# Second layer of a mixture of experts: one third of its token tiles by seven half-width products

## The chip, the cores and the metric

The kernel runs on one NeuronCore of a Trainium2 chip. Its engines run their own instruction queues in order: TensorE (PE: matmuls, with their weight loads shown apart as PEld), VectorE (DVE), ScalarE (ACT), GpSimd (POOL) and SyncE (SP), which here issues the DMAs. Matmul results land in PSUM, eight banks of 128 partitions x 2 KB; GpSimd works on SBUF alone in this kernel. The metric is the device time of one execution in microseconds (us), the median over runs.

## What is computed

Two parts follow each other. The first is a gated linear recurrence over 768 tokens for 4 batches of 8 heads of 48; the second a dense mixture of 8 experts over the 3072 tokens of 384 features that come out of it:

```python
for t in range(S):
    state = f[:, :, t, :, None] * state + np.einsum('bhd,bhe->bhde', k[:, :, t], v[:, :, t])
    y[:, :, t] = np.einsum('bhd,bhde->bhe', q[:, :, t], state)
...
for e in range(E):
    h = np.maximum(x @ w1[e], 0.0)
    ye = h @ w2[e]
    out += P[:, e:e + 1] * ye
```

x has 384 features, h has 1024, and P comes from the gate by eight rounds of normalising rows and columns. All inputs are 32-bit. The kernel keeps that precision with 16-bit matmuls by splitting each operand into a high and a low 16-bit part and taking three products: high x high, low x high, high x low. So one exact-looking product of two blocks is three matmuls.

## The kernel before

**Stages.** From 0 to some 490 us the recurrence runs, with experts 0 and 1 as fillers (`raw_pairs`, `moe_tile`, `moe`), and then the gate's normalising rounds. From 492 us to the end 48 steps run, and the change lies in them. A step n is one entry of `ORDER`: an expert e of 2 to 7, a half m of its 1024 hidden features (512, in two blocks c of 256 as they are stored, each again two blocks f of 128), and a batch b of 768 tokens. The tokens of a batch are two halves v of 384, each three tiles t of 128; a matmul of the first layer takes tile t of both halves together, 256 columns.

**First layer of a step (`period`).** h = x @ w1 for three row blocks of features by two of hidden units by three of tokens would be 18 block products; here it is 15, a fast matrix multiplication. `SLOTS` lists them: product number, bank (A to F), whether the bank is begun anew. Each slot issues 6 matmuls of 256 columns (two c, three split parts). What is to be combined between products is in `EVENTS`: after slot s a bank is copied to SBUF by ScalarE ('copy'), VectorE adds a copy to a bank in place ('add') or writes bank plus copy to a new copy ('sum'), and when a bank is complete ScalarE writes its positive part in 16 bits ('hh') and VectorE the remainder ('hl'). The six banks end as the six (f, t) blocks of h: A (0,0), B (1,0), E (0,1), D (1,2), F (0,2), C (1,1). Events past slot 14 run in the first slots of the next step (`pending`). The sums of weight blocks are made by GpSimd in `prepare_w1`, those of x in `convert`.

**Second layer (`layer2`).** For each tile t and half v a result of 128 tokens x 384 features is summed in one PSUM bank over f, c and the three split parts: 12 matmuls of 384 columns; six results, 72 matmuls a step. Two banks (pool `psm`) alternate. When a result is complete it is scaled by its token's P and added to the accumulator `acc`, either by VectorE from PSUM in one instruction, or by ScalarE into SBUF and then GpSimd; two of six go the first way. This generator belongs to the step before: while step n runs its slots, `period` draws 72/15 matmuls of step n-1's second layer behind each slot. In the first step there is none, and the last one's run alone at the end.

**Other work in the slots (`plan`).** Each (n, s) can hold jobs: the next group's weights (`prepare_w1`: load, GpSimd sums, three high parts on ScalarE, three low parts on VectorE; `prepare_w2`: load, one high part of 768 columns, two low parts of 384), the results of experts 0 and 1 that were stored early and are added back (`readds`, line 1137, on VectorE or on ScalarE and GpSimd), and checks of the inputs' range (`all_checks`, line 1155: it loads all 64 weight blocks once more and takes their largest value on VectorE, then samples q, k and v in `guard`, then `verdict`). If a check fails, `general`, a slow form, runs behind the fast one.

**Order.** `mm` (line 277) chains all matmuls in the order of the program and `pin` does so for each other engine, so no engine takes an instruction ahead of an earlier one. An instruction waits for what it reads, and a bank or tile is written anew only when its readers are done; readers of one bank on two engines also go one after the other.

Of the kernel before, what the change touches and what calls it, by code (L numbers as in the profile page):

```python
# [19 lines left out]
C = 64  # L20
HS = S // 2
# [22 lines left out]
XW1_MAX = 65000.0 / DM  # L44
W2_MIN, W2_MAX = 2.0 ** 4, 2.0 ** 15
# [27 lines left out]
ORDER = [(e, m, b) for e in range(2, NE) for m in range(2) for b in range(B)]  # L73
STEPS = 8
# [175 lines left out]
def fast(ctx, tc, qkf, vbd, wg, w1, w2, out, flag):  # L250
# [83 lines left out]
    def load(e, k, j):  # L334
        src = (w1 if k == 1 else w2)[e, j]
        n = 4 * (k - 1) + j
        if n < 6:
            raw = xp.tile([128, 1152], F32, name=f"w{k}r_{e}_{j}", tag=f"x{'hl'[n % 2]}{3 - n // 2}", bufs=1)[:, 0:768]
        else:
            raw = rp.tile([128, 768], F32, name=f"w{k}r_{e}_{j}", tag="wraw")  # L340
# [430 lines left out]
    def guard():  # L771
# [8 lines left out]
        def load_qk(n):  # L780
            t = lp.tile([128, 768], F32, name=f"qks{n}", tag="wmax", bufs=2)[0:R, 0:512].rearrange("r (i m t) -> r i m t", i=8, m=2)
# [5 lines left out]
        def load_v(n):  # L787
            t = lp.tile([128, 768], F32, name=f"vs{n}", tag="wmax", bufs=2).rearrange("s (i e) -> s i e", i=8)
# [7 lines left out]
        before = None  # L796
        for n in range(9):
            now = (load_qk if n < 4 else load_v)(n % 4) if n < 8 else None
            if before:
                pin(nc.vector.tensor_reduce(out=before[1], in_=before[0], axis=AX.X, op=ALU.max, apply_absolute_value=True))  # L800
            before = now
            yield
# [194 lines left out]
    k1, k2 = {}, {}  # L997

    def prepare_w1(e, j):
        raw = rp.tile([128, KT, 256], F32, name=f"k1r_{e}_{j}", tag="wraw")  # L1000
        nc.sync.dma_start(out=raw, in_=w1[e, j])
# [9 lines left out]
        for r, p, op, q in WSUMS:  # L1011
            pin(nc.gpsimd.tensor_tensor(out=block(r), in0=block(p), in1=block(q), op=ALU.add if op == '+' else ALU.subtract))  # L1012
# [15 lines left out]
    def prepare_w2(e, j):  # L1028
        raw = rp.tile([128, 2, DM], F32, name=f"k2r_{e}_{j}", tag="wraw")
        nc.sync.dma_start(out=raw, in_=w2[e, j])  # L1030
        yield
        wh, wl = (lp.tile([128, 2, DM], F16, name=f"k2{n}_{e}_{j}", tag=f"k2{n}", bufs=4) for n in "hl")
        pin(nc.scalar.activation(out=wh, in_=raw, func=AF.Copy, scale=W2S))
        yield
        for g in range(2):
# [3 lines left out]
            yield  # L1039

# [62 lines left out]

    def layer2(n, h):
# [3 lines left out]
        for t in range(TT):  # L1108
            for v in range(2):
                u = 2 * b + v  # L1110
                ps = psm.tile([128, DM], F32, name=f"kyps_{n}_{t}_{v}", tag="m")
                i = 0
                for f in range(2):
                    for c in range(2):
                        wh, wl = k2[e, 2 * m + c]
                        hh, hl = h[f, t]
                        for a, w in ((hh, wh), (hl, wh), (hh, wl)):
                            mm(out=ps, lhsT=a[:, c, 128 * v:128 * v + 128], rhs=w[:, f, :], start=(i == 0), stop=(i == 11))
                            i += 1
                            if i < 12:  # L1120
                                yield
                y = acc[b][:, v, t, :]
                p = pes[:, u * TT + t, e:e + 1]
                if n == first[b]:
                    pin(nc.scalar.activation(out=y, in_=ps, func=AF.Copy, scale=p))
# [29 lines left out]
    def all_checks():  # L1155
        todo = [(e, j, k) for e in range(NE) for k in (1, 2) for j in range(4)]
        raws_ = []
        for i in range(len(todo) + 1):
# [8 lines left out]
            yield  # L1167
        yield from guard()
        yield from verdict()

    plan = {}

    def at_slots(n, slots, gen):
# [142 lines left out]
```

## Time and profile before

| what | value |
|---|---|
| median of 3 runs | 1544.53 us (1544.12 to 1544.67) |
| span of the profiled execution | 1542.9 us |
| instructions | 32479 |
| TensorE clock over the span, mean granted | 0.996 of full speed |

The profile gives no other time of the profiled execution than its span, from its first to its last instruction; the runs' median is 1.6 us longer.

```profile
core 0: 1542.9 us, clock 0.996
```

How to read it: busy time is the union of an engine's instructions, in us, with its share of the span. A matmul's record covers its way through the array, so records of successive matmuls overlap, and the distance from start to start is what a matmul costs in a full queue. Rows of groups give line, engine, operation, what is written from what by the program's names (kyps is a result of the second layer, kb_A a bank of the first, kh and kl the two parts of h, k1 and k2 the weights of the two layers, cp a copied bank, yt and acc an evicted result and the accumulator), shapes, count, then busy us, mean ns of one, and idle time of the engine before it with what ended it. Line 278 is the helper that issues every matmul.

### The profile page before, as it was taken

To read this page: it belongs to the slowest core of one execution; us is meant where nothing else is said; L and a number is where in the kernel's file an instruction comes from. 1 tells how busy PE (TensorE), PEld (TensorE's weight loads), DVE (VectorE), ACT (ScalarE), POOL (GpSimd) and SP (SyncE) were. 2 spreads that over 40 slices of the span, in tenths; PEclk is the share of its full clock that TensorE was granted. 3 is DMA by queue.
4 is the path that set the end of the run, shared out by engine and by line. 5 is a ranking of instruction groups with operands and counts; after the bars stand their busy time and mean duration, and the time that the engine had idled before them with its cause. 6 is when DMAs were issued, how large, how long until landed. Compare 5 with 4: busy or idle time off the path is not lost.

```text
span 1542.9 us, 32479 instructions
## 1 busy us (share of the span) xinstructions
PE 1518.7 (98%) x13454; PEld 1104.3 (72%) x13454; DVE 1091.6 (71%) x1810; ACT 775.2 (50%) x1489; POOL 517.0 (34%) x656
## 2 busy tenths in 40 slices
PE   7999999999999999999999999999999999999998
PEld 5788876676666777777777777777777777777775
DVE  8888888984774667666767677666766666665554
ACT  6655556553344655555544554445444454445432
POOL 1244434545527112333333332222322232222211
PEclk9999999999999999999999999999999999999999
DMA  9455555531002122222222222111212112100011
GB/s 270 113 134 133 124 137 122 141 95 29 32 32 78 31 83 78 69 87 67 83 73 88 72 78 63 52 62 42 64 50 62 44 39 57 31 12 11 6 57 65
DMA packets 89678, 114.39 MB, mean 74 GB/s; under 512 B 50640, under 2 KB 67152, under 8 KB 89520
## 3 DMA queue, kind: packets, MB, share of 16 engines
q1 hardware_dynamic: 89520, 112.22, 26.1%
q8 instruction: 107, 1.75, 0.5%
q14 instruction: 51, 0.42, 0.1%
HBM read 88.41 MB, written 14.16 MB: 66 GB/s over the span
## 4 chain that ended last, share of the span: by engine, by line
PE 91%; DVE 5%; ACT 2%; POOL 1%; issue 1%; DVEq 0%; ACTq 0%; POOLq 0%
PE kyps L278 36%; PE yps L278 12%; PE hps L278 9%; PE kb_A L278 8%; PE kb_B L278 8%; PE kb_D L278 6%; PE kb_C L278 4%; PE kb_E L278 2%; PE kb_F L278 2%; PE kvps L278 1%; PE aps L278 1%; POOL xs L965 1%; PE wps L278 0%; DVE w2l L350 0%; POOL k1s L1012 0%
## 5 line engine op out<-in xcount | busy, mean ns | idle before, releaser
L1131 POOL TENSOR_TENSOR acc<-acc,yt 128x384 f32<-128x384 f32 x172 | 173.3, 1008 | 629.7 <-ACT yt L1130 629.7
L278 PE MATMUL kyps<-k2h,kl 128*128 128x384 f16 x1152 | 375.6, 326 | 0.0
L278 PE MATMUL kyps<-k2h,kh 128*128 128x384 f16 x1152 | 375.6, 326 | 0.0
L278 PE MATMUL kyps<-k2l,kh 128*128 128x384 f16 x1152 | 375.6, 326 | 0.0
L278 PEld LDWEIGHTS <-k1h 128*128 128x128 f16 x2880 | 281.5, 98 | 70.4
L278 PEld LDWEIGHTS <-kh 128*128 128x128 f16 x2304 | 225.4, 98 | 103.9
L1130 ACT ACTIVATE yt<-kyps,pes 128x384 f32<-128x384 f32 x172 | 99.8, 580 | 323.0 <-PE kyps L278 321.1
L278 PEld LDWEIGHTS <-k1l 128*128 128x128 f16 x1440 | 140.7, 98 | 63.2 <-issue 5.7
L1127 DVE SCALAR_TENSOR_TENSOR acc<-kyps,pes,acc 128x384 f32<-128x384 f32 x92 | 56.8, 617 | 171.7 <-PE kyps L278 171.7
L278 PEld LDWEIGHTS <-kl 128*128 128x128 f16 x1152 | 112.7, 98 | 44.7
L1224 ACT ACTIVATE cp<-kb_A 128x512 f32<-128x512 f32 x144 | 86.0, 597 | 86.0 <-PE kb_A L278 85.4
L278 PE MATMUL yps<-w2h,hl 128*128 128x384 f16 x384 | 125.8, 328 | 3.1 <-DVE hl L431 3.0
L278 PE MATMUL yps<-w2l,hh 128*128 128x384 f16 x384 | 125.9, 328 | 1.0 <-DVE w2l L350 1.0
L278 PE MATMUL yps<-w2h,hh 128*128 128x384 f16 x384 | 125.8, 328 | 0.2 <-ACT hh L428 0.2
L278 PEld LDWEIGHTS <-w1h 128*128 128x128 f16 x1344 | 97.1, 98 | 35.2 <-issue 4.3
L1224 ACT ACTIVATE cp<-kb_B 128x512 f32<-128x512 f32 x144 | 87.0, 604 | 50.3 <-DVE kb_B L1226 50.2
L278 PEld LDWEIGHTS <-hh 128*128 128x128 f16 x768 | 74.7, 98 | 47.3 <-issue 2.3
L1229 DVE TENSOR_TENSOR cp<-kb_D,cp 128x512 f32<-128x512 f32 x144 | 98.7, 685 | 12.8 <-PE kb_D L278 11.8
L278 PE MATMUL hps<-xh,w1h 128*128 128x128 f16 (+1 forms) x672 | 83.6, 257 | 1.6 <-DVE hl L382 1.5
L278 PE MATMUL hps<-xl,w1h 128*128 128x128 f16 (+1 forms) x672 | 84.0, 257 | 1.1 <-DVE xl L640 0.6
L278 PE MATMUL hps<-xh,w1l 128*128 128x128 f16 (+1 forms) x672 | 84.6, 257 | 0.1
L278 PE MATMUL kb_A<-xbh,k1h 128*128 128x256 f16 x288 | 78.5, 273 | 0.2 <-ACT cp L1224 0.2
(244 smaller groups left out, 3439.4 us busy)
## 6 DMA issues: line engine op xcount, KB each, us to landing
wm<-in_w_dram SPq DMA_DIRECT2D x64, 384.0 KB, 3.1
q<-in_qkf_dram SPq DMA_DIRECT2D x23, 672.0 KB, 5.4
vr<-in_vbd_dram SPq DMA_DIRECT2D x24, 384.0 KB, 3.6
ys<-yr SPq DMA_DIRECT2D x48, 192.0 KB, 2.8
k1r<-in_w_dram SPq DMA_DIRECT2D x24, 384.0 KB, 3.0
k2r<-in_w_dram SPq DMA_DIRECT2D x24, 384.0 KB, 3.0
yb<-ys SPq DMA_DIRECT2D x48, 192.0 KB, 2.4
out_dram<-acc SPq DMA_DIRECT2D x24, 192.0 KB, 1.9
```

The source lines that it names most:

```text
L278: ins = (nc.tensor.transpose if transpose else nc.tensor.matmul)(**kw)
L965: pin(nc.gpsimd.tensor_tensor(out=block(r), in0=block(p), in1=block(q), op=ALU.add if op == '+' else ALU.subtract))
L1127: pin(nc.vector.scalar_tensor_tensor(out=y, in0=ps, scalar=p, in1=y, op0=ALU.mult, op1=ALU.add))
L1130: pin(nc.scalar.activation(out=yt, in_=ps, func=AF.Copy, scale=p))
L1131: pin(nc.gpsimd.tensor_tensor(out=y, in0=y, in1=yt, op=ALU.add))
L1224: pin(nc.scalar.activation(out=fresh(ev[2]), in_=bk, func=AF.Copy))
L1229: pin(nc.vector.tensor_tensor(out=fresh(ev[4]), in0=bk, in1=old, op=ALU.add if ev[2] == '+' else ALU.subtract))
```

## The change

The middle token tile, t = 1, of each step is taken out of the plain scheme. Its 256 tokens (two halves v) by 256 hidden units of a c block (two f) are seen as a 2 x 2 block matrix A, and the weights, two f by two halves of the 384 features (192 each), as a 2 x 2 block matrix B. The eight block products of A B become seven, with four sums of blocks of A, four of B, and sums of the products. Three split parts and two c each: 42 matmuls of 192 columns take the place of 24 of 384. The other two tiles stay as they were: 48 matmuls of 384.

- *Left sums*: when bank E (f = 0, t = 1) is complete, ScalarE writes its positive part as 32-bit ('hs') and the high part of block A11 ('ga'); VectorE makes four sums of blocks from the banks E and C and SBUF ('gs'), and A11's low part ('gb'); ScalarE writes the sums' high parts ('gh') and GpSimd their low parts ('gl'). E's own 'hh' and 'hl' go.
- *Right sums*: `prepare_pairs` loads each w2 block a second time, makes four sums of 192 columns on GpSimd, a high part of 768 columns on ScalarE and a low one on VectorE, once in four steps for each c.
- *Results* (`paired`): two banks hold two half-width sums each. Three are copied by ScalarE to SBUF, GpSimd makes two sums of the copies, VectorE one from PSUM, and these are added to the banks in PSUM by VectorE (192 columns for one half v, 384 for the other), after which the two results are evicted; the second one's add and eviction come one and two slots later.
- *Order of the second layer*: plain results (0, 2) first, then the pair. It begins at slot 2 of the next step (`LAG`), not at slot 0, and is drawn by units: a plain matmul counts 1, a narrow one 0.51, and a pause of 5 at the end. In the last step the pair comes before the last plain result, and banks of the first layer serve as rooms.
- *Plan*: all early results go by ScalarE and GpSimd; the weights' largest values are taken from the blocks that are loaded anyway (experts 0 and 1 are loaded for it in `first_maxima`); slots of the weight preparation move; the verdict moves to the last four steps. In a slot a step's own events now come before those left from the step before.
- Two limits of the checks are halved, since sums of blocks are larger, and the buffers for raw weights become three.

```diff
+          14: (('sum', 'D', '-', 4, 3), ('hs', 'E'), ('hh', 'D', 1, 2)), 15: (('add', 'C', '+', 3), ('ga', 'E'), ('hh', 'C', 1, 1), ('gs', 'E', 0)),
+          16: (('gs', 'C', 1), ('gs', 'E', 2), ('gs', 'C', 3)), 17: (('hl', 'C', 1, 1), ('add', 'F', '+', 10)),
+          18: (('gh', 0, 2), ('hh', 'F', 0, 2)), 19: (('gl', 0, 2), ('hl', 'F', 0, 2)), 20: (('gh', 2, 4), ('hl', 'D', 1, 2)), 21: (('gl', 2, 4), ('gb', 'E'))}
...
+        def product(out, left, right, start=False, stop=False):
+            for c in range(2):
+                if left is None:
+                    a = [x[:, c, :] for x in h['a']]
+                elif left[0] is None:
+                    a = [x[:, left[1], c, :] for x in h['g']]
...
+                for i, (x, y) in enumerate(((a[0], w[0]), (a[1], w[0]), (a[0], w[1]))):
+                    mm(out=out, lhsT=x, rhs=y, start=start and c == 0 and i == 0, stop=stop and c == 1 and i == 2, skip_group_check=True)
+                    yield PAIR_COST
+
+        def paired(t=PAIRED):
...
+            yield from product(x0, None, (0, 0), start=True)
+            yield from product(x1, (None, 1), (None, 1))
+            copy(0, x0)
+            yield from product(y0, (None, 0), (None, 0), start=True)
+            copy(1, x1)
+            yield from product(y1, (None, 2), (None, 2))
+            copy(2, y0)
+            pin(nc.gpsimd.tensor_tensor(out=part[:, 1, :], in0=part[:, 1, :], in1=part[:, 2, :], op=ALU.add))
+            pin(nc.gpsimd.tensor_tensor(out=both[:, 1, :], in0=part[:, 0, :], in1=part[:, 1, :], op=ALU.add))
+            yield from product(x0, (1, 0), (1, 0))
+            pin(nc.vector.tensor_tensor(out=both[:, 0, :], in0=y1, in1=part[:, 0, :], op=ALU.add))
+            yield from product(x1, (None, 3), (1, 1), stop=True)
+            yield from product(y0, (1, 1), (None, 3), stop=True)
+            pin(nc.vector.tensor_tensor(out=x1, in0=x1, in1=both[:, 0, :], op=ALU.add))
+            evict(t, 0, px, True)
+
+            late = n < len(ORDER) - 1
+            postpone(late, lambda: pin(nc.vector.tensor_tensor(out=py, in0=py, in1=both, op=ALU.add)))
+            postpone(2 * late, lambda: evict(t, 1, py, False))
+            yield PAUSE
...
-            at_slots(n, (0, 2, 7, 11, 13), gen)
-            at_slots(n + 1, (5, 6, 8), gen)
+            at_slots(n, (0, 5, 5, 6, 9, 11, 13), gen)
+            at_slots(n + 1, (11, 13, 14) if not n % 4 else (4, 6, 8), gen)
...
+        elif kind == 'gs':
+            f, n = hs['f'], ev[2]
+            v, other, op = ((1, 4, ALU.subtract), (1, 5, ALU.add), (0, 1, ALU.subtract), (0, 2, ALU.add))[n]
+            pin(nc.vector.scalar_tensor_tensor(out=f[:, n], in0=bk[:, :, 128 * v:128 * v + 128], scalar=0.0, in1=f[:, other], op0=ALU.max, op1=op))
...
+            for ev in EVENTS.get(s, ()):
+                event(ctxt, ev)
             for ev in pending.pop(0) if pending else []:
                 event(*ev)
-            for ev in EVENTS.get(s, ()):
-                event(ctxt, ev)
+            due()
             for job in plan.pop((n, s), []):
                 job()
-            for _ in range(72 * (s + 1) // PRODUCTS - 72 * s // PRODUCTS):
-                next(lower, None)
+            if s == LAG and n:
+                lowers.append(layers.pop(0))
+            drain((24 * len(PLAIN) + 42 * PAIR_COST + PAUSE) / PRODUCTS)
```

262 lines of the change are left out of this document (183 added, 79 removed), and 2 rows, old and new, of the table EVENTS.

## The prediction, made before the change was run

> **What bounds the kernel now.** I read the busy shares first, then the chain that ended last, then TensorE's own waits in the stage that changes, then that stage in windows.
>
> ```profile
> span 1542.9 us, 32479 instructions
> PE 1518.7 (98%) x13454; PEld 1104.3 (72%) x13454; DVE 1091.6 (71%) x1810; ACT 775.2 (50%) x1489; POOL 517.0 (34%) x656
> PE 91%; DVE 5%; ACT 2%; POOL 1%; issue 1%; DVEq 0%; ACTq 0%; POOLq 0%
> PE kb_A L278 <- ACT cp L1224: 0.7, 3, 0.3
> PE kb_C L278 <- ACT cp L1224: 0.2, 1, 0.2
> 700.00:900.00 200.00, 199.80 (x1493) 145.78 (x1492) 140.62 (x222) 104.48 (x198) 72.69 (x101) 1.00 0.25 75
> 900.00:1100.00 200.00, 200.00 (x1501) 146.60 (x1500) 136.87 (x216) 97.19 (x182) 61.55 (x90) 1.00 0.20 59
> 1100.00:1300.00 200.00, 200.00 (x1503) 146.72 (x1501) 134.68 (x216) 95.59 (x180) 53.18 (x77) 1.00 0.19 53
> ```
>
> TensorE is busy 98% of the span and makes 91% of the chain. The two wait rows are all that it waited from 560 us to the end: 0.9 us. In the three windows (length, then busy time of PE, weight loads, VectorE, ScalarE, GpSimd, then clock) it is never idle, at full clock. So in the 48 steps time is a sum of matmul issue intervals; the other engines only have to keep up. They were busy 412, 297 and 187 of these 600 us.
>
> **What the narrower matmuls save.** A busy TensorE hides the interval, so it is read from starts and from merged pieces.
>
> ```profile
> 1523.15 12.53 PE kyps L278 x77
> 135.84 0.83 PE L278 MATMUL hps<-xh,w1h 128*128 128x128 f16 x12
> 136.51 0.83 PE L278 MATMUL hps<-xl,w1h 128*128 128x128 f16 x12
> 899.93 0.27 PE L278 MATMUL kb_B<-xah,k1h 128*128 128x256 f16 x1
> 900.47 0.27 PE L278 MATMUL kb_B<-xal,k1h 128*128 128x256 f16 x1
> ```
>
> 384 columns: 12.53/77 = 162.7 ns. 128 columns, each with another weight tile: (136.51-135.84)/12 = 55.8 ns. 256 columns: five intervals in 0.54 us, 108 ns. A matmul of 192 columns is not in the trace; halfway between 55.8 and 108 lies 82 ns, and the three known widths lie on one line, so I take 82.3. Bounds: 56 (no narrower than 128) and 108 (no wider than 256). A step has 90 matmuls of 256 columns and 72 of 384; the change turns 24 of the latter into 42 of 192: 24 x 162.7 - 42 x 82.3 = 3905 - 3457 = 0.448 us. Over 48 steps that is **21.5 us**, if nothing new waits.
>
> **A rule against it.** The Trainium skill, page "TensorE: Matmul & The Clock Gate", section "Back-to-back issue gap", says that in a stream of weight-load and matmul pairs one matmul costs about 81 ns at 128 columns and 131 ns at 512. By a line through these figures, an estimate, 42 half widths would cost 1.0 us a step more than 24 full ones. The rows above say 55.8 ns at 128 columns and 162.7 at 384, so here the trace speaks against that rule.
>
> **What the other engines gain in work.** Rows that price it:
>
> ```profile
> L278 PE MATMUL kyps<-k2h,kh x1152: 322/326/327, 505.0 to 1535.0; 128*128 128x384 f16 x192
> L1234 DVE SCALAR_TENSOR_TENSOR kl<-kb_E,kh 128x512 f16<-128x512 f32 x48 | 32.6, 679 | 0.0
> L1127 DVE SCALAR_TENSOR_TENSOR acc<-kyps,pes,acc 128x384 f32<-128x384 f32 x92 | 56.8, 617 | 171.7 <-PE kyps L278 171.7
> L1036 DVE SCALAR_TENSOR_TENSOR k2l<-k2r,k2h 128x384 f16<-128x384 f32 x48 | 26.2, 547 | 0.0
> L1023 DVE SCALAR_TENSOR_TENSOR k1l<-k1r,k1h x48: 410/548/1079, 452.6 to 1426.7; 128x256 f16<-128x256 f32 x24, 128x384 f16<-128x384 f32 x24
> L1149 DVE SCALAR_TENSOR_TENSOR acc<-yb,pes,acc 128x384 f32<-128x384 f32 x19 | 14.5, 766 | 1.3 <-POOL acc L1131 1.3
> L1224 ACT ACTIVATE cp<-kb_A 128x512 f32<-128x512 f32 x144 | 86.0, 597 | 86.0 <-PE kb_A L278 85.4 <-DVE kb_A L1226 0.3
> L1033 ACT ACTIVATE k2h<-k2r 128x768 f16<-128x768 f32 x24 | 20.4, 850 | 0.0
> L1152 ACT ACTIVATE yz<-yb,pes 128x384 f32<-128x384 f32 x29 | 17.6, 606 | 0.0
> L1131 POOL TENSOR_TENSOR acc<-acc,yt 128x384 f32<-128x384 f32 x172 | 173.3, 1008 | 629.7 <-ACT yt L1130 629.7
> L1012 POOL TENSOR_TENSOR k1s<-k1r,k1s 128x128 f32<-128x128 f32 x120 | 56.0, 467 | 3.8
> L737 POOL TENSOR_TENSOR al<-am,ah x21: 1157/1267/1678, 82.7 to 360.9; 128x512 f16<-128x512 f32 x21
> 1004.48 0.68 DVE L1234 SCALAR_TENSOR_TENSOR kl<-kb_E,kh 128x512 f16<-128x512 f32 x1
> 1005.07 0.68 DVE L1234 SCALAR_TENSOR_TENSOR kl<-kb_D,kh 128x512 f16<-128x512 f32 x1
> ```
>
> VectorE, per step: four left sums and the low part of A11, 256 columns at 0.41 each (the least of L1023), +2.05; the low part of E goes, -0.68; two half-width adds at 0.34 (410 less 64 columns at the 1.05 ns of (679-547)/128), +0.68; the full add in PSUM, +0.62; the low part of the paired weights, 768 columns in one step of two, about 0.95/2, +0.48; 19 early results move to ScalarE and GpSimd, -0.30. Together +2.85. The 64 weight maxima stay as many. A step now: from the first kyps at 505.0 to 1535.2 lie 47 steps and 72 matmuls more (11.7 us), so 21.67 us. Before: 412/600 x 21.67 = 14.9; after 17.7 of 21.2, 84%. A left sum reads PSUM and writes 32-bit; at most it costs the 0.62 of 384 columns, which would add 1.0 more (89%).
> ScalarE: E as a wide copy and a 256-column head for its high part (+0.4), two high parts of 512 (+1.2), three copies of 192 (about 0.35 each, +1.05), half a paired weight (+0.43), 0.4 early results (+0.24): +3.3 on 10.7, 66%. GpSimd: two low parts of 512 at 1.27, two half adds at 0.60 (between 467 and 1008), four weight sums of 0.60 every other step, 0.4 early results: +5.3 on 6.8, so 57%.
> No engine passes TensorE in the sum. DMA falls: the 64 weight loads that served the maxima alone become 24 for the pairs and 16 for the first two experts.
>
> **Where a queue could be late.** Order is pinned, so what counts is slack at the places where TensorE needs a bank again. A slot is 21.0/15 = 1.40 us (90 x 108 + 48 x 162.7 + 42 x 82.3 = 21.0). Queued VectorE work starts 0.59 us apart (1004.48, 1005.07), 0.09 below its duration.
> (a) Slots 0 to 5. VectorE now queues, ahead of the add into A: add C, a left sum, the x1 add and its eviction, three more left sums, the full add, low of C, add F. That is 0.60+0.33+0.27+0.5+1.2+0.5+0.6+0.6 = 4.6 us from the start of slot 0, and 0.5 where it must wait for the last pair product. The add starts near 5.1; the chain from there:
>
> ```profile
> 494.99 0.71 DVE kb_A L1226
> 495.72 0.61 ACT cp L1224
> 496.37 0.82 PE kb_A L278 x6
> ```
>
> 1.38 us from add to matmul: 6.5 against slot 5 at 7.0, slack 0.5 us. The low part of C ends near 4.6 against slot 4 at 5.6.
> (b) Slots 4 to 7 where a w2 block is prepared (two steps of four): ScalarE runs the first eviction (ready 6.8), a high part, the w2 high part (0.85 alone, 0.73 queued) and an early result before the copy of A that slot 7 needs: it ends near 9.6, slot 7 starts at 9.8. Slack 0.2 us.
> (c) Slots 9 and 10: copy of B at 11.7 against 12.6, the sum in D at 13.05 against 14.0.
> GpSimd's worst step (n%4 = 0) has 18 us of work; its sums for the last full add come 2 us into the next step, where VectorE reaches that add at 3.4.
> So steady steps should hold, barely. I charge 0.06 us a step, **+3 us**, bounds 0 and 20 (0.4 a step); a gain is excluded, since only 0.9 us of waits are there to lose.
>
> **Ends.** Start: the chain rows above are the first step, where no second layer covers the copies.
>
> ```profile
> 492.74 0.66 PE kb_A L278 x6
> L98 DVE TENSOR_REDUCE gd_r<-gd_t x5: 279/279/280, 1376.2 to 1463.2; 1x1 f32<-1x128 f32 x5
> 1535.77 0.62 DVE acc L1127
> ```
>
> From 492.7 to 505.0 TensorE does 90 matmuls worth 9.8 us: 2.5 lost. The second layer now starts two slots later, so two more slots run bare, with more VectorE work in them: +1.5 (0 to 4). The five verdict transposes take a bank of the two that the second layer alternates; before, no wait of TensorE shows at them; now they fall in other slots, and each that falls inside a result makes the next wait for an eviction (0.6 to 0.8): +2 (0 to 4). Tail: 77 matmuls ran without a wait, then one eviction of 0.62. Now the left sums of the last step (four at 0.41, two low parts of 0.68 on VectorE, behind three adds and three low parts) are ready about 1 us after TensorE gets there, and one result ends by an add, a ScalarE copy and a GpSimd add, 0.8 us after the last plain one: +2 (0.8 to 4).
>
> **Sum.** -21.5 + 3 + 1.5 + 2 + 2 = -13. On the profiled span: 1529.9. The runs' median of 1544.53 lies 1.6 above that span; I keep this: **1531.5**.
>
> **Rivals.** *All hidden*: slack holds, ends cost 2: 1525. For it: TensorE waited 0.9 us in a thousand before, with similar queues. Chance 0.22. *Half eaten*: 0.15 us more a step: 1538.7, 0.10. *No change*: 0.27 more: 1544.5, 0.08.
> *Held by GpSimd* (slower): the low parts of weights read two SBUF tensors, and
>
> ```profile
> 558.25 0.99 POOL L1153 TENSOR_TENSOR acc<-acc,yz 128x384 f32<-128x384 f32 x1 [7.48 <-ACT yz L1152]
> 558.45 1.55 DVE L1023 SCALAR_TENSOR_TENSOR k1l<-k1r,k1h 128x256 f16<-128x256 f32 x2
> ```
>
> two of them, 0.41 + 0.55, took 1.55 us beside a GpSimd add of 0.99: VectorE stood for 0.6. GpSimd goes from 31% to 57%. Two such holds in the three steps of four that split weights are 1.2 us; less a slack of 0.3 that is 0.9 x 36 = 32 us of TensorE waiting at slots 7 and 9: 1544.5 - 21.5 + 5.5 + 32 = 1560. It decides from 0.33 us a step, (21.5-5.5)/48. Against it: the step at 558 lost nothing by the hold. 0.13.
> *Weight loads bind*: a load shows as 98 ns,
>
> ```profile
> L278 PEld LDWEIGHTS <-kh 128*128 128x128 f16 x2304 | 225.4, 98 | 103.9
> ```
>
> and if that were the floor, 42 x 98 = 4.12 beside 3.905: +0.21 x 48 = +10, with ends and queues 1563. The 55.8 ns at 128 columns with new weights each time is against it: 0.02. The rule of the Trainium skill weighed above is this rival with a higher price, some 48 us more than before by its figures, an estimate.
> That the fallback runs because bounds were halved can be left out: for the reference's inputs the largest |x| x 32 x |w1| is 0.40, the new limit 32000/384/64 = 1.30.
>
> **Chances and range.** Forecast (1528 to 1537) 0.45, with the five above 1.00. Faster by over 0.2% (3.1 us, about what a measurement of this kernel can tell from no change): 0.22+0.45+0.10 = 0.77; within 0.08; slower 0.13+0.02 = 0.15. The range leaves out the slower cases and 0.03 below: 1522 to 1545.
>
> **What would show it.** Right: 192-column matmuls 82 ns apart, a step of 21.2 to 21.3 us (21.7 now), VectorE near 82%, TensorE's waits in the stage under 10 us, named ACT cp or DVE cp. Wrong: waits on the copies of A and B in every step (slack mis-sized), low parts of k1l stretched past 1 us often (held), intervals near 98.

## The result, and the profile after

| | before | after |
|---|---|---|
| median of 4 runs, us | 1544.6 (1544.12 to 1544.82) | 1529.22 (1529.12 to 1529.85) |
| span of the profiled execution, us | 1542.9 | 1527.4 |

The ratio is 0.9902, with a 95% interval of 0.9888 to 0.9916: faster by 15.4 us, where the prediction had 13. The head of the page of after, with its line of the chain that ended last:

```profile
span 1527.4 us, 35370 instructions
PE 1497.6 (98%) x14318; PEld 1157.6 (76%) x14318; DVE 1233.7 (81%) x2150; ACT 913.3 (60%) x1823; POOL 766.1 (50%) x964
PE 77%; DVE 13%; ACT 5%; issue 3%; POOL 0%; DMA 0%; DVEq 0%; POOLq 0%; ACTq 0%
```

TensorE has 864 matmuls more, is 21 us less busy, and stands at the same 98%. Its share of the chain fell from 91% to 77%: the chain now often runs through VectorE. That is not 23% of time lost. The chain goes back to whatever released an instruction last, even if the instruction was late by a tenth of a microsecond. What was lost is told by TensorE's own waits from 505 to 1500 us (times in total, how often, the longest) and by the same three windows as before:

```profile
PE kb_A L285 <- ACT cp L1341: 3.1, 7, 0.9
PE kb_B L285 <- ACT cp L1341: 0.9, 1, 0.9
PE kyps L285 <- DVE gd_r L105: 0.4, 1, 0.4
PE kb_C L285 <- DVE kl L1367: 0.4, 1, 0.4
PE gd_t L285 <- ACT yt L1204: 0.2, 1, 0.2
```

```profile
700.00:900.00 200.00, 199.62 (x1685) 158.76 (x1683) 171.02 (x290) 135.99 (x271) 127.40 (x165) 1.00 0.24 70
900.00:1100.00 200.00, 199.08 (x1691) 159.15 (x1689) 164.00 (x292) 122.22 (x245) 106.00 (x147) 1.00 0.12 37
1100.00:1300.00 200.00, 199.50 (x1703) 160.12 (x1701) 162.61 (x283) 123.18 (x248) 100.81 (x140) 1.00 0.12 37
```

The waits sum to 5.0 us. In the windows VectorE rises from 412 to 498 of 600 us (83%), ScalarE from 297 to 381 (64%), GpSimd from 187 to 334 (56%); TensorE, never short of work before by more than 0.2 us in a window, now loses 0.4 to 0.9.

Waits alone undercount. A matmul's record is 0.25 to 0.33 us long but costs 0.08 to 0.16, so TensorE can be late by up to some 0.17 us and no idle time shows. The loss has to be read from start to start. With the trace's own distances (192 columns 82.4 ns, 256 columns 108.7, 384 columns 162.5), a step of after is 90 x 108.7 + 48 x 162.5 + 42 x 82.4 ns = 21.04 us; the shortest steps took 21.09. What a step takes beyond such a sum is called its lateness here. Summed over the 48 steps, TensorE was late by 11.2 us before and by 17.5 us after. That gives the whole account:

| what | us |
|---|---|
| 24 x 162.5 - 42 x 82.4 ns = 0.439 us, 48 times | -21.1 |
| lateness of TensorE in the 48 steps (17.5 - 11.2) | +6.3 |
| the first step's start, 492.57 before and 491.37 after | -1.2 |
| from the last matmul to the end, 7.28 before and 7.77 after | +0.5 |
| sum; the spans differ by 15.5 | -15.5 |

### The profile page after: what moved, and what is told of

It is laid out like the page before. It is cut to its first block, busy times and chain, and to the rows that moved or that the text cites. A ratio compares the mean times of both kernels' runs of the same rounds, so it can differ in the third digit from the quotient of the medians.

```text
span 1527.4 us, 35370 instructions
## 1 busy us (share of the span) xinstructions
PE 1497.6 (98%) x14318; PEld 1157.6 (76%) x14318; DVE 1233.7 (81%) x2150; ACT 913.3 (60%) x1823; POOL 766.1 (50%) x964
## 4 chain that ended last, share of the span: by engine, by line
PE 77%; DVE 13%; ACT 5%; issue 3%; POOL 0%; DMA 0%; DVEq 0%; POOLq 0%; ACTq 0%
PE kyps L285 23%; PE yps L285 13%; PE hps L285 10%; PE kb_A L285 7%; PE kb_B L285 6%; PE kb_D L285 5%; PE kxps L285 4%; PE kb_C L285 3%; PE kb_E L285 2%; PE kb_F L285 2%; PE kvps L285 1%; DVE kf L1354 1%; DVE cp L1346 1%; ACT kh L1364 1%; ACT cp L1341 1%
## 5 line engine op out<-in xcount | busy, mean ns | idle before, releaser
L1205 POOL TENSOR_TENSOR acc<-acc,yt 128x384 f32<-128x384 f32 x175 | 177.7, 1015 | 310.6 <-ACT yt L1204 310.3
L285 PE MATMUL kyps<-k2h,kh 128*128 128x384 f16 x768 | 250.4, 326 | 0.4 <-DVE gd_r L105 0.4
L285 PE MATMUL kyps<-k2h,kl 128*128 128x384 f16 x768 | 250.4, 326 | 0.0
L285 PE MATMUL kyps<-k2l,kh 128*128 128x384 f16 x768 | 250.4, 326 | 0.0
L285 PEld LDWEIGHTS <-kh 128*128 128x128 f16 x1920 | 186.4, 98 | 67.2
L1362 POOL TENSOR_TENSOR kgl<-kf,kgh 128x512 f16<-128x512 f32 x94 | 110.1, 1171 | 22.3 <-ACT kgh L1360 15.6
L285 PEld LDWEIGHTS <-kl 128*128 128x128 f16 x960 | 93.9, 98 | 32.5 <-issue 0.6
L1346 DVE TENSOR_TENSOR cp<-kb_D,cp 128x512 f32<-128x512 f32 x144 | 98.8, 686 | 16.7 <-PE kb_D L285 15.5
L1343 DVE TENSOR_TENSOR kb_C<-kb_C,cp 128x512 f32<-128x512 f32 x96 | 66.6, 694 | 34.4 <-ACT cp L1341 34.3
```

The lines of the kernel that those rows point to most:

```text
L285: ins = (nc.tensor.transpose if transpose else nc.tensor.matmul)(**kw)
L1205: pin(nc.gpsimd.tensor_tensor(out=y, in0=y, in1=yt, op=ALU.add))
L1343: pin(nc.vector.tensor_tensor(out=bk, in0=bk, in1=copies[ev[3]], op=ALU.add if ev[2] == '+' else ALU.subtract))
L1346: pin(nc.vector.tensor_tensor(out=fresh(ev[4]), in0=bk, in1=old, op=ALU.add if ev[2] == '+' else ALU.subtract))
L1362: pin((nc.vector if tag == str(PERIODS - 1) else nc.gpsimd).tensor_tensor(out=hs['g'][1][:, ev[1]:ev[2]], in0=hs['f'][:, ev[1]:ev[2]], in1 ...
```

## The experiments

A step's length in what follows is the distance between the first matmuls of two steps. A loss "at slot 4" or "behind slot 4" lies between that slot's matmuls and the first one of slot 5. All kernels were timed beside the kernel before; the ratios are to it. The last four columns are steps 24 to 40, by n%4:

| kernel | step 1 | steps 2 to 5 | n%4 = 0 | 1 | 2 | 3 |
|---|---|---|---|---|---|---|
| before | 22.50 | 21.56 to 21.62 | 21.60 | 21.60 | 21.60 | 21.60 |
| after | 23.07 | 21.66 | 21.09 | 21.37 | 21.30 | 21.09 |
| e3, first pair result on VectorE | 23.07 | 21.21 to 21.41 | 21.09 | 21.37 | 21.30 | 21.09 |
| e4, one pair's high part later | 23.47 | 21.66 | 21.09 | 22.03 | 21.30 | 21.09 |
| e4b, both pairs' high parts later | 21.99 | 21.66 | 21.09 | 21.09 | 21.09 | 21.09 |
| e5, low parts of w1 earlier | 23.82 | 21.66 | 21.09 | 22.40 | 21.09 | 21.09 |
| e7, left low parts on VectorE | 23.26 | 21.66 | 21.09 | 21.97 | 21.30 to 21.79 | 21.33 |
| e8, all moves | 21.98 | 21.09 | 21.09 | 21.09 | 21.09 | 21.09 |
| e9, no later begin | 22.27 | 21.16 to 22.29 | 21.94 | 21.53 | 22.94 | 21.87 |
| e10, no pause | 22.65 | 22.49 to 23.00 | 22.54 | 22.54 | 22.71 | 22.54 |

**e1: the kernel before with the sums of w1's blocks in two jobs.** The change also cut GpSimd's sums of the next weights in two; here that is done alone.

```diff
-        for r, p, op, q in WSUMS:
-            pin(nc.gpsimd.tensor_tensor(out=block(r), in0=block(p), in1=block(q), op=ALU.add if op == '+' else ALU.subtract))
-        yield
+        for part in (WSUMS[:5], WSUMS[5:]):
+            for r, p, op, q in part:
+                pin(nc.gpsimd.tensor_tensor(out=block(r), in0=block(p), in1=block(q), op=ALU.add if op == '+' else ALU.subtract))
+            yield
...
-            at_slots(n, (0, 2, 7, 11, 13), gen)
+            at_slots(n, (0, 2, 2, 7, 11, 13), gen)
```

> The kernel before, with one thing of the change: the GpSimd sums of the first layer's weights are issued as two jobs of five instead of one of ten. Theory: the 1.2 us by which the 48 steps begin earlier after the change (491.4 us for 492.6) come from this alone, since it lets VectorE's and TensorE's work between the two jobs go on: the first kb_A starts near 491.3, the run takes 1543.3. Rival: they come from the third raw buffer or from chance: the first kb_A stays at 492.5 and the run at 1544.6.

Measured: 1543.05 us, ratio 0.9990 (0.9981 to 1.0000), span 1542.0, first step at 491.34. So the 1.2 us that the account has ahead of the stage belong to a side effect: in the traces of all kernels with two jobs the first step begins at 491.26 to 491.37, in the two with one job (before and e2) at 492.57 and 492.59. TensorE's waits from 300 to 495 us, of before and then of e1, say where they were:

```profile
PE hps L278 <- DVE hl L382: 1.5, 3, 1.0
```

```profile
PE hps L278 <- DVE hl L382: 0.3, 1, 0.3
```

A low part of the fillers' h was late in the kernel before; the row of after is the same as e1's, but for its line numbers. Why GpSimd's shorter jobs free that VectorE instruction was not followed further.

**e2: the kernel before with the middle tile in eight half-width products.** As many multiplications as before, each matmul of 384 columns cut in two.

```diff
-                            mm(out=ps, lhsT=a[:, c, 128 * v:128 * v + 128], rhs=w[:, f, :], start=(i == 0), stop=(i == 11))
+                            for d in ((slice(0, DM),) if t != 1 else (slice(0, DM // 2), slice(DM // 2, DM))):
+                                mm(out=ps[:, d], lhsT=a[:, c, 128 * v:128 * v + 128], rhs=w[:, f, d], start=(i == 0 and d.start == 0), stop=(i == 11 and d.stop == DM), skip_group_check=True)
```

> The kernel before, with the middle tile's 24 matmuls of 384 columns as 48 of 192, so eight half-width block products in place of seven. Theory: 48 x 82.4 - 24 x 162.5 = 0.055 us a step more, 2.6 us in all: 1547.2. So narrowing alone gains nothing, and the gain of the change is the six matmuls left out in each step. Rival (weight loads of 98 ns bind when they follow each other): 48 x 98 - 24 x 162.5 = 0.80 us a step, 38 us: 1583.

Measured: 1547.46 us, ratio 1.0018 (1.0008 to 1.0027); steps of 21.66 where before has 21.60, that is 24 x (2 x 82.4 - 162.5) = 55 ns. Narrowing costs 2.3 ns a pair and no more, though the weight loads in the tile doubled (14606 in the whole run against 13454). The rival *Weight loads bind* falls, and the gain comes from 42 products instead of 48 alone.

**e3: the pair's first result on VectorE in every step.** In steps that write an accumulator for the first time, the result went to ScalarE.

```diff
-                pin(nc.scalar.activation(out=y, in_=ps, func=AF.Copy, scale=p))
+                if direct and t == PAIRED:
+                    pin(nc.vector.tensor_scalar(out=y, in0=ps, scalar1=p, scalar2=None, op0=ALU.mult))
+                else:
+                    pin(nc.scalar.activation(out=y, in_=ps, func=AF.Copy, scale=p))
```

> The changed kernel; in the four layers that write the accumulator for the first time, the pair's first result is evicted by VectorE and not by ScalarE. Theory: the 0.57 us that steps 2 to 5 each lose at slot 1 (the copy of A stands behind this eviction, which waits for VectorE's add) go away: these steps fall from 21.66 to 21.1 us, the run from 1529.2 to 1527.1. Rival: ScalarE is late there because VectorE's add of C is late; then one more VectorE instruction in slot 0 makes it worse or leaves it, 1529.2 to 1530.

Measured: 1527.84 us, ratio 0.9891 (0.9875 to 0.9908). The timeline of after (start, duration, engine, line) shows what stood in the way in steps 2 to 5:

```profile
549.68 0.58 ACT L1199 ACTIVATE acc<-kxps,pes 128x384 f32<-128x384 f32 x1
550.16 0.59 ACT L1341 ACTIVATE cp<-kb_A 128x512 f32<-128x512 f32 x1
550.12 0.27 PE L285 MATMUL kb_B<-xbl,k1h 128*128 128x256 f16 x1
...
550.80 0.27 PE L285 MATMUL kb_A<-xah,k1h 128*128 128x256 f16 x1 [0.41 <-ACT cp L1341]
```

ScalarE's eviction stands ahead of the copy of A; TensorE could have begun A anew at about 550.23, had to wait for the copy's end at 550.75, and so is late by 0.57. With the eviction on VectorE steps 2 and 3 drop to 21.21. Steps 4 and 5 gained less, 21.41 and 21.37, because other losses came to light behind slot 4: in step 5 that of the next experiment, in step 4 a check of the inputs' range, 0.45 us of small instructions on VectorE (from 572.61 in e3) ahead of the add into A. So the run gained 1.4 us and not the 2.1 expected.

**e4 and e4b: the high part of the pairs' weights later.** In steps of n%4 = 1 after loses 0.27 us behind slot 4. ScalarE, VectorE and TensorE there, in after:

```profile
851.25 0.83 ACT L1068 ACTIVATE k2sh<-k2s 128x768 f16<-128x768 f32 x1
851.98 0.62 ACT L1360 ACTIVATE kgh<-kf 128x512 f16<-128x512 f32 x1
852.50 0.59 ACT L1364 ACTIVATE kh<-kb_F 128x512 f16<-128x512 f32 x1
852.98 0.60 ACT L1341 ACTIVATE cp<-kb_A 128x512 f32<-128x512 f32 x1
...
851.84 0.69 DVE L1343 TENSOR_TENSOR kb_A<-kb_A,cp 128x512 f32<-128x512 f32 x1
...
853.18 0.33 PE L285 MATMUL kyps<-k2l,kh 128*128 128x384 f16 x1
853.63 0.27 PE L285 MATMUL kb_A<-xbh,k1h 128*128 128x256 f16 x1
```

The add into A ends at 852.53 as planned, but ScalarE takes up the copy only at 852.98, behind 0.83 us of weights. The next matmul was due 0.16 after 853.18 and came 0.45 after it. e4 moves that job (c = 0), e4b the other one (c = 1) as well:

```diff
-            for c, slots in enumerate((((n - 1, 11), (n - 1, 12), (n - 1, 13), (n, 2), (n, 4)), ((n, 3), (n, 4), (n, 5), (n, 7), (n, 10)))):
+            for c, slots in enumerate((((n - 1, 11), (n - 1, 12), (n - 1, 13), (n, 4), (n, 5)), ((n, 3), (n, 4), (n, 5), (n, 7), (n, 10)))):   # e4
+            for c, slots in enumerate((((n - 1, 11), (n - 1, 12), (n - 1, 13), (n, 4), (n, 5)), ((n, 3), (n, 4), (n, 5), (n, 9), (n, 10)))):   # e4b
```

> The changed kernel; the high part of the first paired weight block on ScalarE moves from slot 2 to slot 4 of the steps with n%4 = 1, its low part on VectorE from slot 4 to 5. Theory: these steps lose 0.28 us at slot 4, because this high part (0.83 us) stands ahead of the high parts of f and of F and of the copy of A that slot 5 waits for; behind that copy it costs nothing: the steps fall from 21.37 to 21.1, eleven of them, the run to 1526.2. Rival: VectorE's add into A is what is late there; then the step stays at 21.37 and the run at 1529.2.

> As the run before (high part of the first paired block at slot 4), and the second block's high part from slot 7 to 9. That run took away the 0.27 us at slot 4 of the steps with n%4 = 1, but put 0.9 at slot 8: the second block's sums wait for the buffer that the first's low part reads, and its high part at slot 7 stood ahead of the copy of B. Theory: behind that copy it costs nothing: these steps 21.1 us, the run 1526.2. Rival: the chain of the pair's weights is too long in any order, and the loss moves once more, to slots 10 to 12: 1529 or more.

e4 measured 1535.62 us, ratio 0.9944 (0.9927 to 0.9961): the loss behind slot 4 was gone, and 0.9 us behind slot 8 took its place. The expectation was wrong, because it looked at one engine. In after the two blocks of pair weights hang on one chain through three engines:

```profile
683.51 0.95 DVE L1070 SCALAR_TENSOR_TENSOR k2sl<-k2s,k2sh 128x768 f16<-128x768 f32 x1
...
684.53 1.14 POOL L1062 TENSOR_TENSOR k2s<-k2rs 128x192 f32<-128x192 f32 x2 [0.92 <-DVE k2sl L1070]
685.64 0.99 POOL L1205 TENSOR_TENSOR acc<-acc,yt 128x384 f32<-128x384 f32 x1
686.59 1.26 POOL L1065 TENSOR_TENSOR k2s<-k2s,k2rs 128x192 f32<-128x192 f32 x2
...
687.88 0.84 ACT L1068 ACTIVATE k2sh<-k2s 128x768 f16<-128x768 f32 x1 [2.06 <-POOL k2s L1065]
688.63 0.58 ACT L1341 ACTIVATE cp<-kb_B 128x512 f32<-128x512 f32 x1
```

The second block's sums need the buffer that the first block's low part still reads; their high part needs the sums; and the copy of B stands behind that high part on ScalarE. In after the copy comes just in time. Counted from the start of the step (676.67 in after, 676.99 in e4), e4 made the first block's sums 0.7 us later, and the copy with them (12.65 us for 11.96); slot 8 came 0.28 earlier, as the loss behind slot 4 was gone. e4b takes the copy out of the chain by putting the high part behind it, and measured 1524.06 us, ratio 0.9868 (0.9851 to 0.9884), 2.1 us below its expectation: steps 24 to 40 are all at 21.09, since the loss behind slot 1 in steps of n%4 = 2 also went, and step 1, which is one of n%4 = 1, lost 1.1 us less. In after the late copy of B holds up VectorE's queue from slot 9 on into the next step: the add of C in step 10 began 0.40 us after that step's start, in e4b 0.09.

**e5: the low parts of w1 earlier in steps of n%4 = 1,** to bring VectorE's add of C, which it reached late in the next step, forward.

```diff
-            at_slots(n + 1, (11, 13, 14) if not n % 4 else (4, 6, 8), gen)
+            at_slots(n + 1, (6, 8, 11) if not n % 4 else (4, 6, 8), gen)
```

> The changed kernel; the three low parts of the first layer's weights in the steps with n%4 = 1 move from slots 11, 13, 14 to 6, 8, 11. Theory: the 0.2 us that the next step (n%4 = 2) loses at slot 1 come from VectorE, which with these low parts is late for the add of C at slot 0, so that ScalarE's copy of A is late: steps n%4 = 2 fall by 0.2, ten of them, the run to 1527.2. Rival (GpSimd holds VectorE): these parts read two SBUF tensors, at slots 6 and 8 they meet GpSimd's sums and low parts, and the step n%4 = 1 loses at slots 8 and 9 what the next one gains: 1529.

Measured: 1537.26 us, ratio 0.9953 (0.9936 to 0.9969). The step of n%4 = 2 dropped to 21.09 as the theory had it, but the step that got the work lost 1.03 us. That is the rival's place (slot 8) at five times its price, and the hold went the other way: VectorE held GpSimd. The same chain of three engines in e5:

```profile
686.06 1.05 DVE L1038 SCALAR_TENSOR_TENSOR k1l<-k1s,k1h 128x640 f16<-128x640 f32 x1
...
686.39 1.59 POOL L1205 TENSOR_TENSOR acc<-acc,yt 128x384 f32<-128x384 f32 x1
687.93 1.72 POOL L1065 TENSOR_TENSOR k2s<-k2s,k2rs 128x192 f32<-128x192 f32 x2
...
689.69 0.84 ACT L1068 ACTIVATE k2sh<-k2s 128x768 f16<-128x768 f32 x1 [3.11 <-POOL k2s L1065]
```

GpSimd's add takes 1.59 where after has 0.99, its two sums 1.72 where after has 1.26, each beside a VectorE instruction that reads two SBUF tensors. That is 1.1 us of hold on GpSimd, which the chain hands to the copy of B. The Trainium skill, page "SBUF — State Buffer", section "Who interferes with whom", says that a VectorE instruction with two SBUF inputs contends with a GpSimd instruction that reads SBUF; these rows agree.

**e6: the w2 high part two slots later.** It tests place (b) of the prediction, whose loss after shows as 0.13 us behind slot 6 in steps of n%4 = 2 and 3 up to step 19.

```diff
-            at_slots(n, (0, 5, 10, 13), prepare_w2(e2, 2 * m2 + c))
+            at_slots(n, (0, 7, 10, 13), prepare_w2(e2, 2 * m2 + c))
```

> The changed kernel; the second layer's high weight part on ScalarE (and the maximum on VectorE) from slot 5 to slot 7 in the steps with n%4 = 2 and 3. Theory: the 0.13 us these steps lose at slot 6 up to step 19, while early results are still added back, are ScalarE's queue ahead of the copy of A (slot 7 waits for it): gone, eight steps, 1.0 us: 1528.2. Rival: the maximum, now behind the add into B, makes the add into C and the sum in D late at slots 9 and 10: 1529 to 1532.

Measured: 1528.20 us, ratio 0.9895 (0.9878 to 0.9911), span 1526.7. Steps of n%4 = 3 up to step 19 went from 21.22 to 21.09. The place was right and its price small.

**e7: the left sums' low parts on VectorE instead of GpSimd.**

```diff
-            pin((nc.vector if tag == str(PERIODS - 1) else nc.gpsimd).tensor_tensor(out=hs['g'][1][:, ev[1]:ev[2]], in0=hs['f'][:, ev[1]:ev[2]], in1=hs['g'][0][:, ev[1]:ev[2]], op=ALU.subtract))
+            pin(nc.vector.tensor_tensor(out=hs['g'][1][:, ev[1]:ev[2]], in0=hs['f'][:, ev[1]:ev[2]], in1=hs['g'][0][:, ev[1]:ev[2]], op=ALU.subtract))
```

> The changed kernel; the low parts of the four left sums on VectorE and not on GpSimd, in all steps: VectorE gets 1.2 us more a step (83 to 89%), GpSimd 2.3 less. Theory (in-order queues with slack below 0.5 us at a few slots): the pieces at slots 4 and 6 stand ahead of the add into B, so steps that also prepare weights there (n%4 = 2 and 3) lose some 0.5 us, the others less: 1534 to 1544. Rival (GpSimd's holds are what costs): fewer holds, the same or faster, 1525 to 1529.

Measured: 1544.08 us, ratio 0.9996 (0.9986 to 1.0006), at the upper end of what was expected: two instructions of about 0.7 us more a step, on an engine that then is busy 87% in the windows (520 of 600 us), give the whole gain back. It is the same place again, the copy of B, in e7:

```profile
684.88 0.95 DVE L1070 SCALAR_TENSOR_TENSOR k2sl<-k2s,k2sh 128x768 f16<-128x768 f32 x1
...
686.34 0.75 DVE L1362 TENSOR_TENSOR kgl<-kf,kgh 128x512 f16<-128x512 f32 x1
...
685.96 1.59 POOL L1062 TENSOR_TENSOR k2s<-k2rs 128x192 f32<-128x192 f32 x2 [2.49 <-ACT yt L1204]
...
690.50 0.58 ACT L1341 ACTIVATE cp<-kb_B 128x512 f32<-128x512 f32 x1
```

This step begins at 677.92 in e7 and at 676.67 in after. Counted from there, the first block's low part starts 0.12 us later than in after and the copy of B 0.62 later, which is the loss behind slot 8 (0.60). Most of it is GpSimd's: its first two sums took 1.59 where after has 1.14, beside the moved low part, which on VectorE reads two SBUF tensors, the contention of e5 again. In steps of n%4 = 2 and 3 no pair's weights are prepared, and there VectorE's queue alone is late: in step 27 the add into B began 11.13 us after the step's start, behind the moved low parts, and 10.56 in after. The copy of B lost 0.24 to 0.58 there. So the theory holds in those steps, and in steps of n%4 = 1 the loss is a hold that neither theory nor rival had in this direction.

**e8: e3, e4b and e6 at once, and the checks' jobs out of slot 1 of the steps with n%4 = 0** (they sample q, k and v; step 20, with six small instructions on VectorE there, took 22.00 in after).

```diff
-            for s in ((1, 5, 6, 10), (), (), ())[n % 4]:
+            for s in ((5, 6, 10, 11), (), (), ())[n % 4]:
```

> The kernel after with four moves at once: first-written pair results scaled by VectorE, the high parts of both pairs' weights in later slots, the w2 high part two slots later, and the four small samples of q, k and v in slots 5, 6, 10, 11 of their step instead of 1, 5, 6, 10. Theory (each loss of the kernel after has its own cause, so the gains add): the moved pairs alone gave 1524.1; steps 2 to 5 give back 0.45 us each (-1.8), the two slot-6 losses of 0.13 us in steps up to 19 go (-1.0), step 20 loses 0.9 less: 1520.4, ratio to the kernel before 0.9843. TensorE's waits in the stage then lie in the first two steps, in steps 45 and 46 and in the tail alone. Rival (the causes share a cover, so that one move takes the slack of another: the w2 high part at slot 7 now stands next to the pair's at slot 9): 1523 or more, with waits on the copy of B named ACT cp.

Measured: 1520.01 us (1519.55 to 1520.89, 5 runs), ratio 0.9841 (0.9827 to 0.9854). The losses had separate causes, and their gains add, though the single sizes came otherwise than expected: steps 2 to 5 gave back 0.57 us each and not 0.45, because the other moves also took what e3 had left in them; step 20 gave back 0.55 and not 0.9, because 0.36 came up behind slot 8. No run has the moved checks alone. TensorE's longest waits from 505 to 1500 us in e8 (two more of 0.2 us follow), and the chain on its page:

```profile
PE kb_A L285 <- ACT cp L1344: 1.3, 2, 0.9
PE kyps L285 <- DVE gd_r L105: 0.4, 1, 0.4
...
```

```profile
PE 89%; DVE 7%; ACT 2%; issue 1%; DMA 0%; POOL 0%; POOLq 0%; DVEq 0%; ACTq 0%
```

VectorE is as busy as in after (81% of the span), and TensorE's share of the chain is back at 89%. TensorE's lateness over the 48 steps is 8.1 us, less than the 11.2 of the kernel before.

**e9: the second layer from slot 0 again.** `LAG = 2` becomes `LAG = 0`.

> The kernel after with the second layer beginning at slot 0 of the next step again and not at slot 2 (LAG 0). It tests the prediction's start term, which put +1.5 us down to two more bare slots. Theory (the later begin costs some 2 us at the start and buys slack for the left sums and the last low parts): the first two steps, now 35.15 us together, get 1 to 2 us shorter, and in each later step the results of tile 2 wait for the low part of block D and the pair for the left sums' low parts, which come two slots earlier than they are ready: at least 0.5 us a step, 1552 or more. Rival (the later begin buys nothing, the parts are ready in time anyway): only the start changes, 1527 to 1528.

Measured: 1562.12 us, ratio 1.0113 (1.0097 to 1.0128). The first two steps together took 34.35 us where after has 35.15; by start-to-start lateness they lost 3.5 instead of 5.1, so the two bare slots are worth 1.5 us (1.06 of it is the wait behind slot 1 of step 1, which is gone). The rest went as expected in size and not in place: no wait for a low part of D or of the left sums, but 33.2 us at one place, as the waits and the timelines of VectorE and ScalarE in e9 show.

```profile
PE kb_A L285 <- ACT cp L1341: 33.2, 43, 1.6
```

```profile
900.60 0.56 DVE L1249 TENSOR_TENSOR kyps<-kyps,both 128x384 f32<-128x384 f32 x1
...
902.28 0.57 ACT L1204 ACTIVATE yt<-kyps,pes 128x384 f32<-128x384 f32 x1
902.74 0.60 ACT L1341 ACTIVATE cp<-kb_A 128x512 f32<-128x512 f32 x1
```

This step begins at 899.67. With the layer two slots earlier, the pair's second add (900.60) stands ahead of the add of C on VectorE, and the pair's eviction (902.28) ahead of the copy of A on ScalarE. TensorE could have gone on at 902.60 and did so at 903.39.

**e10: no pause.** `PAUSE = 5.0` becomes `PAUSE = 0.0`.

> The kernel after with PAUSE 0 instead of 5: the matmuls of the second layer spread evenly to the end of a step's turn, where now some 0.65 us of slots 0 and 1 hold first-layer matmuls alone. Theory (the pause stands for the last pair result's add and eviction, on which the next step's first result waits for its bank): slot 1 gets cover, so that the losses there in steps 2 to 5 and in steps of n%4 = 2 shrink (some 4 us in all at most), but each step's first plain result waits for the pair's eviction, 0.3 to 0.6 us a step: 1539 to 1554, with waits on kyps named ACT or DVE. Rival (the bank is free in time, the pause only bares slot 1): 1525 to 1528 and no waits on kyps.

Measured: 1591.32 us, ratio 1.0306 (1.0290 to 1.0322): theory in kind, but 1.4 us a step and not 0.3 to 0.6. TensorE and VectorE at the end of a pair in e10:

```profile
868.52 0.27 PE L285 MATMUL kb_A<-xal,k1h 128*128 128x256 f16 x1
870.07 0.34 PE L285 MATMUL kyps<-k2h,kh 128*128 128x384 f16 x1 [1.28 <-DVE acc L1201]
...
867.81 0.68 DVE L1367 SCALAR_TENSOR_TENSOR kl<-kb_C,kh 128x512 f16<-128x512 f32 x1
868.40 0.69 DVE L1343 TENSOR_TENSOR kb_F<-kb_F,cp 128x512 f32<-128x512 f32 x1
869.00 0.36 DVE L1245 TENSOR_TENSOR kxps<-kxps,both 128x192 f32<-128x192 f32 x1
869.39 0.62 DVE L1201 SCALAR_TENSOR_TENSOR acc<-kxps,pes,acc 128x384 f32<-128x384 f32 x1
```

The pair's last matmuls move from slot 0 to slot 1, and with them its add and eviction to behind the next slot's VectorE work: a low part and an add of 1.2 us. The expectation had priced the eviction and not the queue ahead of it.

## Where the prediction was right and where not

The likeliest case came true: 1529.2 lies within its 1528 to 1537, below the 1531.5 of the sum. Of the signs that it named, the 82 ns, a step of 21.2 to 21.3 us (21.29 on average from step 2 to 44), VectorE's share and waits under 10 us are there. The sum gave -13 for the span, which came to -15.5. Matmuls, steady queues and start together were 1.6 us worse than predicted, verdict and tail 2.9 better, and a gain of 1.2 had no term, so part of the agreement is errors that cancel. That the steady queues agree in size is luck in part, since their places agree only in half. One by one:

- **Matmuls, -21.5: -21.1.** The width that was not in the trace, in after:

```profile
847.54 0.25 PE L285 MATMUL kxps<-k2h,kgh 128*128 128x192 f16 x1
...
848.28 0.27 PE L285 MATMUL kb_B<-xbh,k1h 128*128 128x256 f16 x1
```

  Nine matmuls of 192 columns in 0.74 us: 82.2 ns each, 82.4 over the whole stage, where 82.3 had been taken. The rule of the Trainium skill (page "TensorE: Matmul & The Clock Gate", section "Back-to-back issue gap"), by whose figures the change would have cost time (the prediction's estimate), does not hold for this stream: e2, with doubled weight loads, shows it too.
- **Steady queues, +3: +3.7** (lateness in steps 2 to 44, 10.6 after and 6.9 before). The size is right, the places half. Place (b) lost 0.13 us and only while early results ran (e6). Place (c), the copy of B for slot 9, lost nothing in steady steps of after, but is where e4, e5 and e7 broke; the prediction saw the copy's slack and not the chain behind it. Place (a) was late by 0.27 in one step of four, where slack 0.5 had been worked out. Two things failed there together: the slot taken as an even 1.40 us, and the chain from the add to the matmul, 1.38 us in the prediction and 1.79 here (851.84 to 853.63), because it leaves out the pair's high part in ScalarE's queue. Either alone would have fitted (4.95 + 1.38 = 6.33 within 6.45, 4.95 + 1.79 = 6.74 within 7.0); e4b takes the second away and the loss is gone. The pause leaves slots 0 and 1 with little second-layer work:

```profile
848.83 0.27 PE L285 MATMUL kb_B<-xbl,k1h 128*128 128x256 f16 x1
848.94 0.27 PE L285 MATMUL kb_A<-xah,k1h 128*128 128x256 f16 x1
```

  Slot 1 is followed by slot 2 without one matmul between. The step begins at 846.89 and slot 5 was due at 853.34, 6.45 us later and not 7.0. VectorE's queue came out as worked out: the add into A began 4.95 us after the step, where 5.1 had been taken. Because slots 0 and 1 are bare, the copy of A that slot 2 needs, which the list of places does not have, is the one that is late in steps 2 to 5 (2.1 of the 3.7 us; e3) and in steps of n%4 = 2; in e10, where these slots are covered, the loss behind slot 1 is gone. Step 20 added 0.7 with its checks. A gain had been excluded, since waits of only 0.9 us were there to lose; by starts the kernel before lost 6.9 in these steps and e8 loses some 2.5, so a gain was possible.
- **Start, +1.5: +2.0** (lateness in steps 0 and 1, 5.1 after and 3.0 before; the prediction read 2.5 for the first step of before, which lost 2.0 by starts, because slot 0 of step 1 also lies before the first result). e9 bears out the term: without the later begin the start loses 1.5 less, 1.06 of it behind slot 1 of step 1. What else happens there had no term. The kernel before also lost 0.97 behind that slot; what in the change takes this old loss away was not followed. New against it are 0.3 behind slot 8 of step 0, whose cause was not followed either, and in step 1 0.5 behind slot 4 and 1.1 behind slot 8. The 1.1 is the chain of the pairs' weights: GpSimd's sums took 1.79 and 2.04 there (at 512.55 and 514.30), where step 9 has 1.14 and 1.26. With the pairs' high parts moved the start loses 1.1 less (e4b), which overlaps with the 1.5. The first step's earlier start, -1.2, was not foreseen: the sum has no term for the two jobs of w1's sums (e1).
- **Verdict, +2, and tail, +2: together +1.1.** In steps 45 to 47 TensorE was late by 1.8 us, before by 1.2, and the end came 0.5 later after the last matmul. The transposes cost 0.9 in steps 45 and 46, and the last step's left sums, 0.8, where about 1 had been charged for them. Taken off is what the prediction had left out: the kernel before lost 0.9 at the copy of A in steps 46 and 47 together, and after does not. Both terms were sized too large, the transposes (0.9 for 2) more than the tail (0.8 and 0.5 for 2). At two of the five a wait of TensorE shows (gd_r and gd_t, 0.6 us together in the rows above); by starts these two are the 0.9. No run took these terms alone.

The one wait of TensorE from 1485 us to the end in after; by starts it is 0.8 us:

```profile
PE kxps L285 <- DVE kgl L1362: 0.6, 1, 0.6
```

The charges for the other engines held. VectorE's windows give 83%, where 84% was worked out, ScalarE 64 for 66%, GpSimd 56 for 57%. The dearest of the new operations, from the groups of after:

```profile
L1362 POOL TENSOR_TENSOR kgl<-kf,kgh 128x512 f16<-128x512 f32 x94 | 110.1, 1171 | 22.3 <-ACT kgh L1360 15.6 <-DVE kb_F L1343 6.7
```

A low part on GpSimd took 1.17 (1.27 taken), a left sum 0.42 (0.41 taken, bound 0.62). One reading of the prediction is off without weight: (679-547)/128 is 1.03 ns, not 1.05.

Of the rivals, *Held by GpSimd* was real as a mechanism and free in the place that it named. In after:

```profile
730.38 1.68 DVE L1038 SCALAR_TENSOR_TENSOR k1l<-k1r,k1h 128x256 f16<-128x256 f32 x2
...
730.14 1.16 POOL L1362 TENSOR_TENSOR kgl<-kf,kgh 128x512 f16<-128x512 f32 x1
```

Two low parts that take 0.88 elsewhere (at 697.21) took 1.68 beside GpSimd. The step, n = 11, took 21.22 us, and the 0.13 that it lost lies behind slot 6, before the hold, and is place (b)'s. e5 and e7 show the same contention, the other way round, where it does cost. *All hidden* at 1525 fell for the kernel as it stands, by the 2 us of steps 2 to 5 and the quarter microseconds of two steps in four; e8, 1520, shows that nothing in the work itself prevents it.

## What to carry to other kernels

Where TensorE is full, price a change of matmul shapes from start-to-start distances, and measure lateness the same way, because gaps shorter than a record show as no wait. Slack has to be worked out from the times at which each slot of the new schedule really starts, a pause included, and along the whole chain of engines: a copy on ScalarE was late because of a weight buffer that VectorE freed late for GpSimd. Compare two runs by the time since the step's start, since earlier losses move everything behind them. Queue work that is not needed soon (a weight's high part, a check) behind the copy that is; three such moves and one eviction given to another engine were worth 9.2 us here, beside 15.4 for the change itself.

## What the runs showed of the hardware

- A matmul's distance was linear in its columns from 128 to 384, with another weight tile each time: 55.8 ns at 128 (before), 82.4 at 192, 108.7 at 256 and 162.5 at 384. Halving a matmul of 384 columns cost 2.3 ns (e2).
- VectorE at 81% of the span (83% in the windows) was hidden behind TensorE almost without loss in e8 (21.09 us a step against 21.04 of matmuls), while after, with the same share in another order, took 9.2 us more. With 87% the whole gain was lost (e7); whether another order could hide that was not run.
- The contention between VectorE and GpSimd went both ways: two of VectorE's low parts from 0.88 to 1.68 us in after; GpSimd's add from 0.99 to 1.59 in e5, and two of its half-width sums from 1.14 to 1.59 in e7.
